# A list scheduler's table of durations: transposing DMAs, float16 splits, small operations and changes of product type

## The chip, the cores and the metric

The kernel runs on one core of a Trainium2 chip. The metric is device time in microseconds of one execution; the table below gives the median of three executions. The core's engines are TensorE (PE, with its weight loads shown apart as PEld), VectorE (DVE), ScalarE (ACT), GpSimd (POOL) and SyncE (SP), whose queue issues the DMAs here. Every engine runs its own instructions in the order in which they stand in the program and waits on semaphores for the others.

## What is computed

Attention over a local window and block summaries, then LayerNorm and a feed-forward network with a residual. B = 4, H = 8, S = 768, D = 64, so the model width is 512; the FFN goes from 512 to 2048 and back.

```python
block, window = (32, 16)
k_sum = k.reshape(B, H, nb, block, D).max(axis=3)
v_sum = v.reshape(B, H, nb, block, D).mean(axis=3)
scores_l = scale * np.matmul(q, k.transpose(0, 1, 3, 2))
mask_l = np.abs(pos[:, None] - pos[None, :]) < window
scores_s = scale * np.einsum('bhsd,bhnd->bhsn', q, k_sum) + np.log(block)
...
a = softmax(concat([where(mask_l, scores_l, -1e9), scores_s]))
x = a @ concat([v, v_sum])                      # heads side by side: (B, S, 512)
xn = (x - mu) / np.sqrt(var + 1e-06) * g_ln
out = x + np.maximum(xn @ w_ch1, 0.0) @ w_ch2
```

## The kernel before

The rows of all batches are cut into 24 tiles T of 128 rows. Attention runs in 48 steps t = 2T + hh, each for four heads of one tile; LayerNorm runs per tile, the FFN per group g of two tiles (12 groups), each in eight sections s = 8g + j of two blocks of 128 hidden columns.

Attention, t < 12 (batch 0): `early_qk` makes the scores s in float32 with products of 64 rows, `softmax` reduces and masks them on DVE and takes the exponential on ACT, `early_transp` turns the probabilities on PE (pp) and `early_pv` makes o. Before the first of them, `fetch_k0` loads the keys, `batch_k` takes their block maxima on DVE (kmax) and `batch_v0` makes the block means of the values as PE products v0 from value loads in_va. Attention, t ≥ 12: `load_q` and `load_k` split queries and keys into float16 halves (qhl; kh on ACT, kl on DVE from the staged ksg), `load_v` the values (v16), `qk` makes s from kh and kl, `softmax` writes p (DVE, with the row minimum mn; POOL scales mn; ACT the exponential), `transp` splits p into p16 on ACT and POOL and turns it with one transposing DMA on SP into pT, `pv` makes o on PE (12 products), reduces it on DVE into x and scales x on POOL. `batch(b)` prepares the next batch: maxima and sums of its keys, queries and values (bst, kmax, vsum, vm, vps), and `batch_vput` copies vsum into the value staging vst with small SP DMAs.

`ln` makes xn on DVE (bn_stats, bn_aggr, one product). `lnT` turns it: for T < 8 with PE transposes (tx), else with 16 transposes of 32x32 blocks on DVE (xn<-xn); ACT then rounds it to xth, and DVE (T < 8) or POOL makes the rest xtl. `g1(s)` makes h with 24 products, three (high·high, low weights, low x) for each of four parts and two blocks; ACT takes the ReLU and the high part hh, DVE the low part hl. `g2(s)` makes a with 12 products for each of the two tiles. An FFN section of group g needs both tiles of the group, that is xth and xtl of tile 2g + 1, whose attention ends with o of step 4g + 3: o19 is the last attention product ahead of h32, o23 of h40. The weights arrive as raw<-in_w (32 loads) and are turned into w on DVE and ACT (`conv_w`, four DVE instructions each, through wf).

Nothing is issued while this is recorded. Class `Plan` (line 68 on) records each operation with its predecessors (`record`), prices it (`cost`: its length in ns on its engine, and for a DMA the time of its transfer), and `issue` makes an order: a list scheduler places each engine's next ready operation by rank. The ranks begin with the longest path to the end plus a random offset of up to ±2000 ns for each step (`SEED`, `SPREAD`; `DRAWS` = 1) and are then taken from the ends of a schedule, forward and backward, `ROUNDS` = 24 times; the best of the forward ones is kept. `WAIT` and `SAME` are the delays between a predecessor and its follower, `ISSUE` = 450 ns the length of a DMA issue on SP, `SWITCH` = 93 ns a charge on PE, `port` makes DVE and POOL operations that read SBUF twice exclude one another in the plan. The instructions stand in the program in the order found, and the scheduler of the framework is off. All of them are issued from line 284, so the rows of the trace name no other line and are told apart by tiles.

Of the kernel before, what the change touches and what calls it, by code (L numbers as in the profile page):

```python
# [15 lines left out]
F32R = mybir.dt.float32r  # L16
F16 = mybir.dt.float16
# [7 lines left out]
P = 128  # L25
# [14 lines left out]
EH = 4  # L40
BS = 3
ROUNDS = 24
SEED, DRAWS = 2, 1
SPREAD = 2000.0
WARMQ = 4
WARMV = 4
# [17 lines left out]
class Plan:  # L64
# [58 lines left out]
    def record(self, engine, op, a, k):  # L123
        on_chip = lambda x: isinstance(x, bass.AP) and x.space != bass.MemoryType.DRAM
        outs = [x for x in (a[0], k.get("accum_out"), *a[7:8]) if on_chip(x)]
        ins = [x for x in (*a[1:7], *k.values()) if on_chip(x)]
        i, after = len(self.ops) - bool(self.joined), {}
        for aps, write in ((ins, False), (outs, True)):
            for x in aps:
                tile, *b = self.box(x)  # L130
                assert self.uses.get(tile, 1), tile
                if tile not in self.uses:
                    self.uses[tile] = []
                    if tile in self.prev:
                        for _, w, j in self.uses[self.prev[tile]]:
                            after[j] = after.get(j, False) or not w
                        self.uses[self.prev[tile]] = None
                elif tile in self.prev:
                    after.setdefault(self.uses[tile][0][-1], False)
                for c, w, j in self.uses[tile]:  # L140
                    if (write or w) and b[0] < c[1] and c[0] < b[1] and b[2] < c[3] and c[2] < b[3]:
                        after[j] = after.get(j, False) or not (write and w)
                self.uses[tile].append((b, write, i))
        busy, moving = self.cost(engine, op, a, k, ins, outs)
        columns = 0
        if engine == "tensor":
            columns = ({'matmul': 4, 'transpose': 2}[op] if ins[-1].dtype == F32 else 1) * math.prod(n for _, n in a[0].ap[1:]) * ins[0].ap[0][1] / P
        if self.joined:
            x = self.ops[i]
            x.calls.append((op, a, k))  # L150
            x.after.update(after)
            x.busy += busy
            x.columns += columns
        else:
            half = engine == "tensor" and ins[0].ap[0][1] == P // 2
            x = SimpleNamespace(engine=engine, calls=[(op, a, k)], after=after, busy=busy, moving=moving, columns=columns, stage=self.stage, port=self.port(engine, op, ins, outs), half=half)
            self.ops.append(x)
        x.after.pop(i, None)
        if self.joined is None:
            self.joined = True  # L160

    def cost(self, engine, op, a, k, ins, outs):

        free = lambda x: math.prod(n for _, n in x.ap[1:])
        n = max(free(x) for x in ins + outs) if engine != "tensor" else free(a[0])
        if engine == "sync":
            x = (outs + ins)[0]
            return self.ISSUE, x.ap[0][1] * free(x) * mybir.dt.size(x.dtype) / (200.0 if "transpose" in op else 360.0)
        if engine == "tensor":
            dt = ins[-1].dtype  # L170
            if dt == F32R:
                return 0.443 * max(n, 256) + 4.5, 0.0
            if dt == F16 or op == "transpose":
                return max((1 if dt == F16 else 2) * n / 2.4 + 3.0, 28.0), 0.0
            return (2 if ins[0].ap[0][1] > D else 1) * max(2 * n / 2.4 + 2.0, 100.0), 0.0
        psum = any(x.space == bass.MemoryType.PSUM for x in ins)
        pointers = sum(1 for x in ins[1:] if free(x) == 1)
        if engine == "scalar":
            extra = ("accum_out" in k) + sum(isinstance(k.get(x), bass.AP) for x in ("scale", "bias"))
            return n / 1.2 + (51 if psum else 93) + 93 * extra, 0.0  # L180
        if engine == "vector":
            fixed = {"transpose": 183, "tensor_tensor_reduce": 158}.get(op, 70)
            return n / (1.92 if op == "tensor_scalar" and not psum else 0.96) + fixed + 61 * (pointers > 0), 0.0
        if op == "tensor_scalar":
            return 180 + n + 61 * pointers + 300 * (n == 1), 0.0
        if op == "tensor_copy":
            return 120 + 3.33 * n, 0.0
        if op == "tensor_tensor":
            shifted = outs[0].offset // outs[0].ap[0][0] != ins[0].offset // ins[0].ap[0][0]
            return 517 if n == 1 else 40 + 2.1 * n + 110 * (shifted or outs[0].dtype == F32R), 0.0  # L190
        return 60 + 0.8 * n, 0.0

    @staticmethod
# [11 lines left out]
    def schedule(self, rank, after, back):  # L205

        count = len(self.ops)
        before = [[] for _ in range(count)]
        left = [len(x) for x in after]
        for i, x in enumerate(after):  # L210
            for j, wait in x:
                before[j].append((i, wait))
        ready, start, end = [0.0] * count, [0.0] * count, [0.0] * count
        free = dict.fromkeys(self.ENGINES, 0.0)
        coming, waiting = ({e: [] for e in self.ENGINES} for _ in range(2))
        ring, warm, columns, tick = 0.0 if back else self.FIRST, False, 0.0, 0.0
        port, half = 0.0, False
        for i in range(count):
            if not left[i]:
                heapq.heappush(coming[self.ops[i].engine], (0.0 if back else 1000.0, i))  # L220
        for _ in range(count):
            t, e = min(
                (free[e] if waiting[e] else max(free[e], coming[e][0][0]), k)
                for k, e in enumerate(self.ENGINES)
                if waiting[e] or coming[e]
            )
            e = self.ENGINES[e]
            while coming[e] and coming[e][0][0] <= t:
                i = heapq.heappop(coming[e])[1]
                heapq.heappush(waiting[e], (rank[i], i))  # L230
            i = heapq.heappop(waiting[e])[1]
            busy, moving = self.ops[i].busy, self.ops[i].moving
            if self.ops[i].port:
                t = port = max(t, port)
                port += busy
            if e == "tensor" and self.ops[i].half != half:
                half, t = self.ops[i].half, t + self.SWITCH
            if e == "tensor" and not back:
                while t >= tick + self.TICK:
                    warm, columns, tick = columns >= 3200, 0.0, tick + self.TICK  # L240
                busy *= 1 if warm else 2
                at, per = t, self.ops[i].columns / busy
                while t + busy >= tick + self.TICK:
                    columns += (tick + self.TICK - at) * per
                    warm, columns, tick = columns >= 3200, 0.0, tick + self.TICK
                    at = tick
                columns += (t + busy - at) * per
            start[i], free[e], end[i] = t, t + busy, t + busy
            if e == "sync":
                ring = max(ring, t if back else t + busy + self.SETUP) + moving  # L250
                if back:
                    free[e] = max(free[e], ring)
                end[i] = ring + (self.SETUP + busy if back else 0)
            for j, wait in before[i]:
                ready[j] = max(ready[j], end[i] + wait)
                left[j] -= 1
                if not left[j]:
                    heapq.heappush(coming[self.ops[j].engine], (ready[j], j))
        return start, end
# [744 lines left out]
```

## Time and profile before

| | |
|---|---|
| three executions, us | 682.6, 681.9, 684.57; median 682.6 |
| profiled execution, own time, us | 682.88 |
| its span, us | 680.8 |
| mean granted TensorE clock | 0.990 |
| PE busy, us (share) | 655.8 (96%) |
| DVE busy, us (share) | 511.7 (75%) |
| ACT busy, us (share) | 369.8 (54%) |
| POOL busy, us (share) | 218.6 (32%) |

The rows of the profile are of one execution. A row of instructions has the start in us, the busy time in us, the engine, line, operation, out<-in by tile names (without their numbers), shape and count, and in brackets the idle time of the engine just before and what ended it. The span starts with the first instruction and ends with the last; some 2.1 us lie around it.

### The profile page before, as it was taken

How to read it: one execution, taken by the hardware profiler on the slowest of the kernel's cores; microseconds unless marked ns; L12 is line 12 of the kernel's file. 1: busy time of each engine (PE TensorE's matmuls, PEld its weight loads, DVE VectorE, ACT ScalarE, POOL GpSimd, SP SyncE). 2: the span in 40 equal slices, each digit the busy share in tenths (PEclk: the TensorE clock that was granted, in tenths of full speed). 3: DMA queues.
4: the chain of work that ended last, by engine and by line, in shares of the span. 5: the costliest groups of instructions: out<-in, count | busy, mean ns of one | idle time of the engine just before them, and what ended most of it. 6: DMA issues, size and time to landing. Idle time of an engine off the chain costs nothing.

```text
span 680.8 us, 13615 instructions
## 1 busy us (share of the span) xinstructions
PE 655.8 (96%) x4641; PEld 577.8 (85%) x4641; DVE 511.7 (75%) x1370; ACT 369.8 (54%) x970; POOL 218.6 (32%) x421
## 2 busy tenths in 40 slices
PE   9959999999999999989999999899999999999998
PEld 6748898888988987878988888798989888989997
DVE  3899989877566899879999888898998574742211
ACT  3936788475566766666666555666664434311110
POOL 4211200233333444634444354355343332310000
PEclk9959999999999999999999999999999999999999
DMA  9990564446564655655664544564543321210000
GB/s 304 362 350 28 147 214 121 146 138 183 141 164 121 176 139 128 170 151 150 172 141 126 141 102 101 126 146 103 144 108 81 84 79 35 55 24 1 32 1 31
DMA packets 109495, 87.89 MB, mean 129 GB/s; under 512 B 63218, under 2 KB 93938, under 8 KB 109427
## 3 DMA queue, kind: packets, MB, share of 16 engines
q1 hardware_dynamic: 109426, 87.04, 47.0%
q8 instruction: 36, 0.59, 0.4%
q14 instruction: 33, 0.26, 0.1%
HBM read 66.27 MB, written 6.29 MB: 107 GB/s over the span
## 4 chain that ended last, share of the span: by engine, by line
PE 43%; DVE 18%; DMA 13%; ACT 6%; issue 6%; POOL 2%; SPq 1%; ACTq 0%; POOLq 0%; DVEq 0%
PE h L284 20%; PE a L284 19%; DVE xn L284 4%; DMA ksg<-in_kt 4%; DMA bst<-in_vs 3%; DVE kl L284 2%; DMA bst<-in_qa 2%; ACT p L284 2%; DVE hl L284 2%; PE s L284 2%; PE o L284 1%; DVE p L284 1%; DVE v L284 1%; DVE vsum L284 1%; DVE x L284 1%
## 5 line engine op out<-in xcount | busy, mean ns | idle before, releaser
L284 PE MATMUL h<-xth,w 128*128 128x256 f32 x1536 | 301.3, 286 | 0.9 <-ACT xth L284 0.7
L284 PEld LDWEIGHTS h<-xth,w 128*128 128x128 f32 x1536 | 246.0, 190 | 4.1 <-ACT xth L284 1.1
L284 PE MATMUL a<-w,hh 128*128 128x512 f32 (+1 forms) x768 | 241.6, 396 | 0.0
L284 PE MATMUL h<-xtl,w 128*128 128x256 f32 x768 | 216.9, 282 | 0.8 <-POOL xtl L284 0.7
L284 PEld LDWEIGHTS a<-w,hh 128*128 128x128 f32 x768 | 135.4, 188 | 24.2 <-issue 0.9
L284 PE MATMUL a<-w,hl 128*128 128x512 f32 (+1 forms) x384 | 149.9, 390 | 0.2 <-DVE hl L284 0.2
L284 PEld LDWEIGHTS h<-xtl,w 128*128 128x128 f32 x768 | 145.8, 190 | 3.3 <-POOL xtl L284 1.0
L284 DVE SCALAR_TENSOR_TENSOR hl<-h,hh 128x512 fp32r<-128x512 f32 x96 | 65.7, 685 | 71.6 <-ACT hh L284 71.0
L284 ACT ACTIVATE hh<-h 128x512 fp32r<-128x512 f32 x96 | 56.5, 588 | 97.3 <-PE a L284 39.3
L284 ACT ACTIVATE p<-p,mn,sv 128x184 f32<-128x184 f32 x144 | 76.5, 532 | 57.7 <-POOL mn L284 57.5
L284 PEld LDWEIGHTS a<-w,hl 128*128 128x128 f32 x384 | 72.2, 188 | 16.9 <-DVE hl L284 0.6
L284 POOL TENSOR_TENSOR p<-p,p 128x512 f16<-128x512 f32 x72 | 71.6, 1002 | 39.6 <-ACT p L284 39.0
L284 DVE STREAM_TRANSPOSE xn<-xn 32x128 f32<-32x128 f32 x256 | 77.5, 303 | 4.5
L284 ACT ACTIVATE kh<-ksg,sv 128x368 f16<-128x368 f32 x72 | 43.2, 599 | 50.5 <-POOL ksg L284 39.3
L284 DVE SCALAR_TENSOR_TENSOR kl<-ksg,sv,kh 128x368 f16<-128x368 f32 x72 | 50.3, 699 | 20.8 <-ACT kh L284 20.0
L284 POOL TENSOR_SCALAR mn<-mn,sv 128x2 f32<-128x2 f32 x72 | 30.7, 427 | 78.5 <-DVE mn L284 69.1
L284 DVE CUSTOM_DVE_ANT_0 p<-s,mask 128x184 f32<-128x184 f32 x144 | 44.7, 340 | 9.9 <-PE s L284 9.2
L284 ACT ACTIVATE bst<-bst 128x384 f32<-128x384 f32 (+2 forms) x55 | 32.5, 590 | 26.8 <-DMA bst<-in_qa 11.6
L284 POOL COPY ksg<-ksum 128x48 f32<-128x48 f32 x72 | 18.8, 261 | 84.1 <-DMA ksg<-in_kt 66.1
L284 DVE SCALAR_TENSOR_TENSOR v<-vst,sv,v 128x256 f16<-128x256 f32 x72 | 42.5, 612 | 1.7 <-ACT v L284 1.2
L284 DVE SCALAR_TENSOR_TENSOR wf<-raw,wf 128x512 uint32<-128x512 uint32 x64 | 41.8, 680 | 0.0
L284 POOL TENSOR_TENSOR x<-x,rc 128x256 f32<-128x256 f32 x36 | 25.2, 699 | 47.6 <-DVE x L284 44.0
(106 smaller groups left out, 818.3 us busy)
## 6 DMA issues: line engine op xcount, KB each, us to landing
raw<-in_w SPq DMA_DIRECT2D x32, 512.0 KB
ksg<-in_kt SPq DMA_DIRECT2D x72, 184.0 KB
qs<-in_qt SPq DMA_DIRECT2D x72, 128.0 KB
out_x<-x SPq DMA_DIRECT2D x23, 256.0 KB
vst<-in_va SPq DMA_DIRECT2D x36, 128.0 KB
bst<-in_ks SPq DMA_DIRECT2D x20, 192.0 KB
bst<-in_qa SPq DMA_DIRECT2D x15, 256.0 KB
bst<-in_vs SPq DMA_DIRECT2D x20, 192.0 KB
```

The source lines that it names most:

```text
L284: getattr(getattr(nc, self.ops[i].engine), op)(*a, **k)
```

## The change

Only the planner's table and the seed of its one draw change; every instruction of the program stays. A transposing DMA is priced at 1500 ns of SP's queue where every DMA was 450. On DVE the fixed part of `tensor_tensor_reduce` falls from 158 to 92 ns, an operation on four columns (rc and its reciprocal) gets 120 ns more, one that writes float16 (kl, v, qhl) 80 more. On POOL `tensor_tensor` gets 60 ns more. `half` had told products over 64 rows from all others; now it tells apart 64 rows (1), float16 (2) and the rest (0), and `SWITCH` is charged at each change of it except from 0 to 2.

```diff
-SEED, DRAWS = 2, 1
+SEED, DRAWS = 7, 1
...
-            half = engine == "tensor" and ins[0].ap[0][1] == P // 2
+            half = engine == "tensor" and (1 if ins[0].ap[0][1] == P // 2 else 2 * (ins[-1].dtype == F16))
...
-            return self.ISSUE, x.ap[0][1] * free(x) * mybir.dt.size(x.dtype) / (200.0 if "transpose" in op else 360.0)
+            return 1500.0 if "transpose" in op else self.ISSUE, x.ap[0][1] * free(x) * mybir.dt.size(x.dtype) / (200.0 if "transpose" in op else 360.0)
...
-            fixed = {"transpose": 183, "tensor_tensor_reduce": 158}.get(op, 70)
-            return n / (1.92 if op == "tensor_scalar" and not psum else 0.96) + fixed + 61 * (pointers > 0), 0.0
+            fixed = {"transpose": 183, "tensor_tensor_reduce": 92}.get(op, 70)
+            return n / (1.92 if op == "tensor_scalar" and not psum else 0.96) + fixed + 61 * (pointers > 0) + 120 * (n == 4) + 80 * (outs[0].dtype == F16), 0.0
...
-            return 517 if n == 1 else 40 + 2.1 * n + 110 * (shifted or outs[0].dtype == F32R), 0.0
+            return 517 if n == 1 else 100 + 2.1 * n + 110 * (shifted or outs[0].dtype == F32R), 0.0
...
             if e == "tensor" and self.ops[i].half != half:
-                half, t = self.ops[i].half, t + self.SWITCH
+                t += self.SWITCH if self.ops[i].half + half != 2 or not self.ops[i].half else 0
+                half = self.ops[i].half
```

The changed kernel issues from line 285. Three places of its order follow, first that of before, then the new one.

DVE at the start, around the second tile's LayerNorm (mv1 and xn3 are of tile 1; tx0 and tx1 are the PE transposes of tiles 0 and 1; wf and w are weights). Before:

```order
L284 TENSOR_TENSOR w2_2_272<-wf2_2_271,w2_2_272 128x512
L284 BN_AGGR mv1_156<-s6_1_155 128x2
L284 TENSOR_SCALAR wf3_1_274<-raw1_3_273 128x512
L284 SCALAR_TENSOR_TENSOR xn3_158<-x1_144,mv1_156,gb_74 128x512
L284 SCALAR_TENSOR_TENSOR wf3_1_274<-raw1_3_273,wf3_1_274 128x512
L284 TENSOR_SCALAR wf4_1_280<-raw1_4_279 128x512
L284 SCALAR_TENSOR_TENSOR wf3_1_274<-raw1_3_273,wf3_1_274 128x512
L284 TENSOR_SCALAR wf3_2_277<-raw2_3_276 128x512
L284 TENSOR_TENSOR xtl_0_132<-tx1_159,xth_0_131 128x4x128
```

Now:

```order
L285 ISA mn5_173 128x1
L285 BN_AGGR mv1_156<-s6_1_155 128x2
L285 TENSOR_SCALAR wf1_2_265<-raw2_1_264 128x512
L285 SCALAR_TENSOR_TENSOR wf2_1_268<-raw1_2_267,wf2_1_268 128x512
L285 SCALAR_TENSOR_TENSOR xn3_158<-x1_144,mv1_156,gb_74 128x512
L285 TENSOR_SCALAR rc5_180<-sum5_174 128x4
L285 TENSOR_TENSOR w1_2_269<-wf2_1_268,w1_2_269 128x512
L285 RECIPROCAL rc5_180<-rc5_180 128x4
L285 SCALAR_TENSOR_TENSOR wf1_2_265<-raw2_1_264,wf1_2_265 128x512
L285 TENSOR_SCALAR wf2_2_271<-raw2_2_270 128x512
L285 TENSOR_TENSOR xtl_0_132<-tx0_133,xth_0_131 128x4x128
```

xn3 now stands three instructions behind the score reductions of step 5 (fourteen before) and ahead of the first tile's xtl; the second tile's xtl follows ten instructions further, sixteen behind xn3 (four before). On PE and SP, ahead of this, of the seven products v0 none stands ahead of the score products s0 now (four before), and two ahead of s1 (all seven before); on SP the last of the four key loads is the sixth transfer (the tenth before), ahead of three value loads in_va that stood before it.

DVE where PE waits for the low keys of step 25 (x11 is the result of step 23, xn69 and xn73 are turned rows of two tiles). Before:

```order
L284 STREAM_TRANSPOSE xn69_751<-xn68_748 32x4x32 x5
L284 SCALAR_TENSOR_TENSOR kl25_0_838<-ksg25_0_836,sv2_728,kh25_0_837 128x368
L284 STREAM_TRANSPOSE xn69_751<-xn68_748 32x4x32 x7
L284 TENSOR_REDUCE x11_768<-o23_783 128x256
L284 SCALAR_TENSOR_TENSOR hl36_672<-h36_670,hh36_671 128x512
L284 STREAM_TRANSPOSE xn69_751<-xn68_748 32x4x32
L284 SCALAR_TENSOR_TENSOR qhl26_858<-qs78_857,sv2_728,qhl26_858 64x512
L284 SCALAR_TENSOR_TENSOR kl25_1_844<-ksg25_1_842,sv2_728,kh25_1_843 128x368
```

Now:

```order
L285 TENSOR_REDUCE x11_768<-o23_783 128x256
L285 SCALAR_TENSOR_TENSOR kl25_0_838<-ksg25_0_836,sv2_728,kh25_0_837 128x368
L285 SCALAR_TENSOR_TENSOR qhl26_858<-qs78_857,sv2_728,qhl26_858 64x512
L285 SCALAR_TENSOR_TENSOR v16_1_352<-vst1_78,sv2_728,v16_1_352 128x4x64
L285 BN_STATS s6_11_785<-x11_768 128x6
L285 SCALAR_TENSOR_TENSOR v16_1_352<-vst1_78,sv2_728,v16_1_352 64x4x64
L285 BN_AGGR mv11_786<-s6_11_785 128x2
L285 SCALAR_TENSOR_TENSOR hl38_678<-h38_676,hh38_677 128x512
L285 SCALAR_TENSOR_TENSOR xn72_788<-x11_768,mv11_786,gb_74 128x512
L285 SCALAR_TENSOR_TENSOR kl25_1_844<-ksg25_1_842,sv2_728,kh25_1_843 128x368
L285 STREAM_TRANSPOSE xn73_789<-xn72_788 32x4x32 x16
```

Tile 11's reduction and LayerNorm have moved ahead of step 25's keys, no transposes of the tile before stand here any more, and the 16 of tile 11 stand in one piece behind kl25_1.

SP around the transposing DMA of step 34 (vst is the value staging, vsum the block sums, ksg staged keys, qs staged queries). Before:

```order
L284 DMA vst1_78<-in_va 128x256
L284 DMA qs121_1177<-in_qt 64x512
L284 DMA vst1_78<-in_vb 32x256
L284 DMA vst1_78<-vsum3_1059 24x128 x2
L284 DMA ksg36_0_1162<-in_kt 128x368
L284 DMA_TRANSPOSE pT_34_1108<-p16_34_1107 128x12x128
L284 DMA ksg36_1_1168<-in_kt 128x368
```

Now:

```order
L285 DMA vst1_78<-vsum3_1059 24x128
L285 DMA_TRANSPOSE pT_34_1108<-p16_34_1107 128x12x128
L285 DMA qs121_1177<-in_qt 64x512
L285 DMA vst1_78<-in_va 128x256
L285 DMA ksg36_0_1162<-in_kt 128x368
L285 DMA qs121_1177<-in_qt 64x512
L285 DMA vst1_78<-in_vb 32x256
L285 DMA vst1_78<-vsum3_1059 24x128 x2
```

The pair of copies from vsum and the load of ksg36_0 have moved from ahead of the transposing DMA to behind it.

On PE, counted in the same way: between the last product of o19 and the first of h32 stood 48 h, 48 a, 16 s and 12 o products and now stand 36, 36, 8 and 12; the corresponding stretches of h40, h48 and h64 are shorter too, while between the last product of s20 and the first of s36 720 h products stand where 648 stood. Blocks of float16 products between others number 103 before and 102 now. The last instructions of every engine are the same.

## Rows read from the trace of the kernel before

**Rows 1.** Stretches (us): length, busy of PE, PEld, DVE, ACT, POOL; PEclk, DMA share, GB/s

```profile
0.00:17.00 17.00, 15.30 (x68) 10.61 (x68) 6.16 (x15) 5.73 (x18) 7.13 (x43) 1.00 0.91 304
34.00:51.00 17.00, 9.72 (x50) 8.20 (x50) 17.00 (x40) 6.67 (x16) 3.10 (x2) 0.60 1.01 351
51.00:255.00 204.00, 201.35 (x1433) 178.24 (x1432) 166.16 (x424) 137.40 (x386) 55.51 (x114) 1.00 0.52 143
255.00:425.00 170.00, 163.43 (x1186) 142.15 (x1185) 153.10 (x435) 106.96 (x269) 77.69 (x134) 1.00 0.55 138
252.28:268.89 16.61, 16.09 (x101) 12.72 (x101) 15.56 (x42) 9.79 (x25) 8.42 (x13) 1.00 0.46 115
```

**Rows 2.** What PE waited for, 255 to 430 us: total us, times, longest

```profile
PE o L284 <- DMA pT<-p: 4.5, 5, 2.2
PE s L284 <- DVE kl L284: 2.5, 4, 1.7
PE h L284 <- POOL xtl L284: 0.7, 1, 0.7
PE vps L284 <- DVE vm L284: 0.5, 1, 0.5
PE s L284 <- ACT kh L284: 0.3, 1, 0.3
PE a L284 <- DVE hl L284: 0.2, 1, 0.2
```

**Rows 3.** What DVE waited for in the first 34 us

```profile
DVE kmax L284 <- DMA spare<-in_ks: 8.8, 4, 4.5
DVE p L284 <- PE s L284: 2.7, 5, 0.9
```

**Rows 4.** DVE instructions at the start, around the second tile's xn and xtl

```profile
41.33 0.74 DVE L284 SCALAR_TENSOR_TENSOR xn<-x,mv,gb 128x512 f32<-128x512 f32 x1
...
43.90 0.69 DVE L284 TENSOR_TENSOR xtl<-tx,xth 128x512 fp32r<-128x512 f32 x1
```

**Rows 5.** PE instructions at the start, the transposes of the second tile

```profile
42.13 1.12 PE L284 MATMUL tx<-ident,xn 128*128 128x128 f32 x4 [5.79 <-DVE xn L284]
```

**Rows 6.** DVE instructions that make kl, a usual one and that of s25_1

```profile
299.46 0.60 DVE L284 SCALAR_TENSOR_TENSOR kl<-ksg,sv,kh 128x368 f16<-128x368 f32 x1 [2.34 <-ACT kh L284]
...
304.99 1.49 DVE L284 SCALAR_TENSOR_TENSOR kl<-ksg,sv,kh 128x368 f16<-128x368 f32 x1
```

**Rows 7.** POOL instruction beside the second of these

```profile
304.79 1.29 POOL L284 TENSOR_TENSOR xtl<-xn,xth 128x512 fp32r<-128x512 f32 x1 [0.38 <-ACT xth L284]
```

**Rows 8.** PE instruction that waited for it

```profile
306.53 0.24 PE L284 MATMUL s<-kl,qhl 128*128 128x184 f16 x1 [1.67 <-DVE kl L284]
```

**Rows 9.** SP's queue ahead of the transposing DMA of step 34

```profile
421.68 1.54 SPq L284 DMA_DIRECT2D vst<-vsum  x2
423.32 0.46 SPq L284 DMA_DIRECT2D ksg<-in_kt  x1
423.89 1.83 SPq L284 DMA_TRANSPOSE pT<-p  x1
```

**Rows 10.** PE instructions of step 34 that waited for it

```profile
428.19 0.74 PE L284 MATMUL o<-v,pT 128*128 128x128 f16 x12 [2.22 <-DMA pT<-p]
```

**Rows 11.** PE instructions: o19, the h32 product that waited, o23

```profile
248.83 0.74 PE L284 MATMUL o<-v,pT 128*128 128x128 f16 x12
...
271.06 0.39 PE L284 MATMUL h<-xtl,w 128*128 128x256 f32 x1 [0.69 <-POOL xtl L284]
...
295.55 0.74 PE L284 MATMUL o<-v,pT 128*128 128x128 f16 x12
```

**Rows 12.** POOL instruction that makes the last xtl ahead of h40

```profile
316.86 1.54 POOL L284 TENSOR_TENSOR xtl<-xn,xth 128x512 fp32r<-128x512 f32 x1 [2.32 <-ACT xth L284]
```

**Rows 13.** The chain of waits, 454 to 463 us: start us, us, what

```profile
454.50 4.28 PE h L284 x36
...
459.12 2.84 PE a L284 x12
```

More of the change, by code (lines that the diff above doesn't have):

```diff
@@ L216, in schedule @@
         ring, warm, columns, tick = 0.0 if back else self.FIRST, False, 0.0, 0.0
-        port, half = 0.0, False
+        port, half = 0.0, 0
         for i in range(count):
```

## The prediction, made before the changed kernel ran

> **What bounds the kernel now.** I read the table of busy time by stretch first. TensorE (PE) is busy nearly everywhere, so the time can only fall where PE stands idle. Its idle time is the length of a stretch less its busy time: 7.3 us between 34 and 51 us (17.00 − 9.72), where the granted clock is 0.60 of full speed on average; 2.7 us between 51 and 255 us, spread over 204 us; 6.6 us between 255 and 425 us [rows 1]. Then I read what PE waited for. Between 255 and 430 us the waits add up to 8.7 us: 4.5 for the transposed probabilities pT that a DMA brings, 2.5 for kl, the low half of the keys that VectorE (DVE) makes, and smaller ones for xtl, vm, kh and hl [rows 2]. (One of them, 2.2 us, lies just behind 425 us [rows 10].) After 430 us the view of waits has no row at all: there PE has products of the FFN to fill every gap. So two places can pay, the start (until the first h product) and the middle, where a wait of PE is a wait of the kernel.
>
> The change alters only the planner's table, so the same instructions run and only their order differs. What each misplaced instruction costs is therefore a question of these two places.
>
> **The start.** PE's idle 5.8 us ends with the transposes tx of the second tile, which wait for xn [rows 5]. On DVE xn runs at 41.33 and the second xtl at 43.90 us [rows 4]; conversions of weights stand ahead of and between them, and DVE is busy all of the 17 us [rows 1]. In the changed order three instructions stand between the last score reduction and xn, where fourteen stood (twelve of them conversions); but sixteen, mostly the same conversions, now stand between xn and the second xtl, where four did. The wait moves from xn to xtl, then, and the first h products come when DVE has done the work ahead of the second xtl. Net work ahead of it, counted from the order: one more weight instruction (0.6), one reduction of kmax (0.5) and two pairs for rc (0.5) less one short conversion (0.3), about +1.3 us, an estimate. Against that DVE idles less before: in the first 34 us it waited 8.8 us for the keys' loads and 2.7 us for score products [rows 3]. The changed order issues the key loads ahead of three value loads of 262 KB each (at the 304 GB/s of the first stretch [rows 1], 2.6 us), and puts the score products s0 and s1 ahead of nearly all products of the block means. Saved idle time: 0 at worst; at best 2.7 and 2.1 of the 2.6 us, that is 4.8; I take 2.6, the loads alone. First h: −2.6 + 1.3 = **−1.3 us**, bounds +1.3 and −3.5.
>
> **The middle, pT.** The longest wait, 2.22 us, is the 12 o products of step 34 waiting for pT_34 [rows 10]. Its transposing DMA takes SyncE's queue from 423.89 for 1.83 us, directly behind two small copies of vsum (1.54 us) and a load of keys (0.46 us) [rows 9]: 2.0 us of queue ahead of the one transfer that is urgent. The changed order puts pT_34 ahead of the pair and of ksg36_0. What is late next is the POOL split that feeds it. I let this wait go but for 0.3 us, and of the other four (2.3 us together) I leave 0.7, since a table that says 1500 instead of 450 makes the planner see the queue blocked: 4.5 becomes 1.0; bounds 0 and 4.5. Behind it stand now qs121, a value load, ksg36_0 and the pair, delayed by at most its 1.83 us; PE waited for none of what these feed but kl and kh [rows 2].
>
> **The middle, kl.** The 1.67 us wait of s25_1 [rows 8] ends with kl25_1, which took 1.49 us where a usual one takes 0.60 [rows 6]. It started at 304.99, and POOL ran xtl from 304.79 to 306.08 [rows 7]: kl moved only when POOL had finished. In the changed order kl25_1 stands behind xn72 and ahead of 16 transposes, and kl25_0 and qhl26 right behind the reduction of x11. I let 2.8 us (kl and kh) become 0.7; bounds 0 and 2.8, and beyond that if POOL's splits now meet more of them.
> The Trainium skill ("SBUF — State Buffer", section "SBUF: two separate sides") says that VectorE and GpSimd take a shared port pair as an exclusive lock for a whole instruction, and the loser blocks fully. The trace agrees: 1.49 against 0.60 us. The new table prices kl at a constant, with no such wait in that number; by the rule the 2.5 us of kl would stay, and the sum would be 678 instead of 676.
>
> **The middle, the LayerNorm chain.** Group 4's first h (h32) must wait for the second tile of its input: from the end of o19 (248.83 + 0.74 = 249.57) to the h32 product that waited for xtl (271.06) are 21.5 us [rows 11]; DVE has of it the stretch from the reduction of x9 at 252.28 to the last transpose at 268.89 us, 42 instructions with 15.56 us of work, 0.37 each [rows 1]. In the changed order 14 instructions of other steps leave that stretch and 3 come: −11 × 0.37 = −4.1 us, so 17.4 us if the rest of the chain stays, and 14.3, an estimate, if the reduction (now 2.7 us behind o19's end) starts at once and half a microsecond of queueing goes. But PE's work between o19 and h32 falls too: 48 h, 48 a, 16 s and 12 o products become 36, 36, 8 and 12. An h product takes 4.28/36 = 0.119 us, an a product 2.84/12 = 0.237 [rows 13]: 17.1 us of these become 12.8, and with the short s and o products, some 0.05 us each, 18.5 becomes 13.7 us. A stall of 0.6 to 3.7 us. For h40 the distance falls from 21.8 to 15.1; its chain, now 22.1 us (296.29 to 318.40) [rows 11, 12], loses ten instructions, 3.7 us, to 18.4 at most. For h48 and h64 the distances become 16.4 and 18.2 us. I take 1.5 us for all four, near the low end, since a chain may also lose its queueing; bounds 0 and 9.2 (3.7 + 3.3 + 2.0 + 0.2 with 18.4 us for the last two).
> What pays for this: between the last product of s20 and the first of s36 stand 720 h products where 648 stood, 8.6 us more FFN work beside the same work of the other engines, so fewer gaps for PE.
>
> Sum of the middle: 8.7 us before; 1.0 + 0.7 + 1.5 and 0.3 for the rest (vm, hl) = 3.5 after: **−5.2 us**, bounds −8.7 and, with the chains at 9.2, +2.5. The 2.7 us between 51 and 255 us [rows 1] I leave as they are (±2). The new rule on product types: changes to and from float16 products number 103 before and 102 after; one fewer is worth at most one product's 0.1 us: **−0.1**. The last instructions of all engines are the same: 0.
>
> The profiled execution took 682.88 us, 680.8 of span and 2.1 around it; it is 0.3 above the median of the runs, 682.6. 682.9 − 1.3 − 5.2 − 0.1 = 676.3; less 0.3 for the median's level: **676.0 us**.
>
> **Rivals.** *Better:* all of the middle's waits go and the start gives its 3.5: 682.6 − 8.7 − 3.5 = 670.4. For it: nothing waited after 430 us, where FFN work is at hand. Against: the four shorter distances.
> *No change:* the waits are of a sort that the table does not hold (kl held up by POOL [rows 6, 7], queues behind a landing transfer), so a new order has new ones of the same size: 682.6 − 1.3 − 0.1 = 681.2, or 682.5 without the start. For it: the table before was no worse in the first 255 us, and PE idled only 2.7 us in 204 there.
> By the rule of the Trainium skill on the port pair (same page and section) the kl part of this rival holds; the trace agrees for kl25_1 [rows 6, 7].
> *Slower:* the LayerNorm chain. If taking instructions out of DVE's stretch shortens the chain only to 20 us, because DVE then waits in the stretch for its inputs, the four stalls are 6.3 + 4.9 + 3.6 + 1.8 = 16.6 instead of 1.5: 676.0 + 15.1 = 691. It decides from a chain of some 18 us (8.8 us of stalls, near 683) and passes 686 at 18.7. For it: 17.4 and 18.4 by the instructions alone; against: the last 3 us of both are queueing, which the order can remove.
> *Not what it says:* the order differs also because the one random draw is another (seed 7, offsets up to ±2000 ns on every step). The rule for float16 changes their number by one, so it does nothing on the chip. The gain may be the draw's, the table's or both; the time would be the same, but each alone would not give it.
>
> **How the numbers follow.** Forecast 0.50, better 0.14, no change 0.23, slower 0.13. A measurement of this kernel can tell about 0.5% from no change: faster is below 679.2, slower above 686.0. The forecast and the better case are nearly all faster, of the no-change case little; a quarter of the slower rival (chain under 18.7) falls inside the bound: faster 0.64, same 0.25, slower 0.11. The range must leave out no more than 0.2: from 669.5 (the better case and 0.9 us of the first 255 us) to 684.0, which takes in no change and the mild end of the chain's stalls.
>
> **What would show it.** In the changed kernel's profile the first h products start when the second xtl has run, near 42.6 us instead of 43.9; PE's wait for pT between 255 and 430 us falls under 1.5 us and that for kl under 1; h waits for xtl at h32 and h40, 0.5 to 3 us each; no waits after 430 us. A single 3 us stall at each of the four groups' first h would make the slower rival right; s waits for kl with kl over 1 us beside a POOL split, the no-change one. A first h later than 44 us would show that the conversions ahead of xtl cost more than the loads gave. What would make all of it wrong is a gap in the first 255 us that the trace of before does not have.

## The result, and the profile after

The changed kernel took 674.28 us, median of four runs (672.41 to 674.73), against 682.25 for the kernel before in the same comparison: a ratio of 0.9872 with a 95% interval of 0.9841 to 0.9902, 8.0 us less. 676.0 had been predicted. Its profiled execution took 674.68 us, with a span of 672.9 and a granted clock of 0.990 on average, as before.

The stretches that answer to [rows 1], with the columns explained there:

```profile
34.00:51.00 17.00, 9.21 (x48) 8.26 (x49) 17.00 (x37) 7.01 (x17) 1.17 (x2) 0.60 0.97 333
51.00:255.00 204.00, 201.33 (x1434) 179.12 (x1432) 163.61 (x421) 135.53 (x379) 59.53 (x112) 1.00 0.52 143
255.00:425.00 170.00, 167.13 (x1206) 147.46 (x1206) 148.38 (x407) 104.02 (x261) 74.73 (x126) 1.00 0.54 131
```

PE is idle 2.9 us between 255 and 425 us where it was 6.6; DVE has 4.7 us less to do there (148.4 against 153.1); that work stands later, beside the last FFN sections (between 510 and 612 us DVE is busy 76.6 us where it was 62.6). The stretch from 51 to 255 us is as before. What PE waited for between 255 and 430 us, answering to [rows 2]:

```profile
PE o L285 <- DMA pT<-p: 1.3, 1, 1.3
PE s L285 <- ACT kh L285: 0.8, 1, 0.8
PE s L285 <- DVE kl L285: 0.4, 1, 0.4
PE a L285 <- DVE hl L285: 0.4, 1, 0.4
```

2.9 us in four waits instead of 8.7 in thirteen. After 430 us there is none, as before. A wait costs more than the idle time listed, since the modelled end of a product lies behind the start of the next in an unbroken row (an h product is listed 0.28 us long, and the next one starts 0.12 us after it). Counted from start to start, the thirteen gaps of before were 10.9 us longer than the usual spacing, the four of after 3.5: **7.4 of the 8.0 us** are here, and the start gives most of the rest.

The start, answering to [rows 4, 5], DVE and then PE:

```profile
34.96 0.75 DVE L285 SCALAR_TENSOR_TENSOR xn<-x,mv,gb 128x512 f32<-128x512 f32 x1
...
43.42 0.69 DVE L285 TENSOR_TENSOR xtl<-tx,xth 128x512 fp32r<-128x512 f32 x1
```

```profile
35.76 0.92 PE L285 MATMUL tx<-ident,xn 128*128 128x128 f32 x4
37.36 0.58 PE L285 MATMUL h<-xth,w 128*128 128x256 f32 x1 [0.68 <-ACT xth L285]
44.17 0.58 PE L285 MATMUL h<-xtl,w 128*128 128x256 f32 x1 [6.22 <-DVE xtl L285]
```

xn comes 6.4 us sooner, the second xtl only 0.5 us. PE's wait moved from tx to the first xtl product and is 6.2 us long instead of 5.8.

### The profile page after: what moved, and what is told of

Its sections match the earlier page's. It is cut to its first block, busy times and chain, and to the rows that moved or that the text cites. A ratio compares the mean times of both kernels' runs of the same rounds, so it can differ in the third digit from the quotient of the medians.

```text
span 672.9 us, 13587 instructions
## 1 busy us (share of the span) xinstructions
PE 652.1 (97%) x4641; PEld 577.5 (86%) x4641; DVE 514.5 (76%) x1370; ACT 370.0 (55%) x970; POOL 225.0 (33%) x421
## 4 chain that ended last, share of the span: by engine, by line
PE 81%; DVE 7%; DMA 6%; ACT 3%; issue 2%; POOL 1%; SPq 1%; ACTq 0%; DVEq 0%; POOLq 0%
PE h L285 35%; PE a L285 34%; PE o L285 5%; PE s L285 4%; DMA pT<-p 1%; DVE xn L285 1%; DMA bst<-in_qa 1%; DVE wf L285 1%; ACT p L285 1%; PE v L285 1%; DMA qs<-in_qt 1%; DMA blk<-in_blocks 1%; SPq L285 1%; PE last L285 1%; DMA ksg<-in_kt 1%
## 5 line engine op out<-in xcount | busy, mean ns | idle before, releaser
L285 ACT ACTIVATE p<-p,mn,sv 128x184 f32<-128x184 f32 x144 | 76.6, 534 | 39.7 <-POOL mn L285 38.9
L285 POOL TENSOR_TENSOR p<-p,p 128x512 f16<-128x512 f32 x72 | 73.6, 1034 | 46.7 <-ACT p L285 46.0
L285 DVE SCALAR_TENSOR_TENSOR kl<-ksg,sv,kh 128x368 f16<-128x368 f32 x72 | 50.3, 699 | 12.4 <-ACT kh L285 11.8
L285 POOL TENSOR_SCALAR mn<-mn,sv 128x2 f32<-128x2 f32 x72 | 25.0, 348 | 77.5 <-DVE mn L285 69.0
L285 ACT ACTIVATE bst<-bst 128x384 f32<-128x384 f32 (+2 forms) x55 | 32.4, 590 | 27.0 <-DMA bst<-in_qa 16.3
L285 DVE SCALAR_TENSOR_TENSOR v<-vst,sv,v 128x256 f16<-128x256 f32 x72 | 44.8, 636 | 0.3
L285 POOL TENSOR_TENSOR x<-x,rc 128x256 f32<-128x256 f32 x36 | 27.4, 762 | 42.7 <-DVE x L285 39.1
```

What stands on the lines that cost most here:

```text
L285: getattr(getattr(nc, self.ops[i].engine), op)(*a, **k)
```

## Experiments: which part of the change did it

The change has three ingredients: the price of a transposing DMA (1500 ns of SP's queue), the other prices, and the draw (seed 7). The first of these is a correction: in the trace of the kernel before, the 36 transposing DMAs hold SP's queue for 1.49 us in the median (1.29 to 2.27). Six runs take the ingredients apart.

**The price of the DMA put back**, all else new:

```diff
-            return 1500.0 if "transpose" in op else self.ISSUE, ...
+            return self.ISSUE, ...
```

> The changed kernel with one number put back: a transposing DMA is planned at 450 ns of SP's queue again; seed 7 and all other new prices stay. Between the last product of s20 and the first of s36 the order then has 612 h products, where the changed kernel has 720 and the kernel before 648. Theory P (pacing: this one number makes the planner space the attention steps wider and put more FFN work between them): the waits of PE between 255 and 430 us come back, 7 us or more, and the time is 681 to 684 us. Rival D (the draw of seed 7 made the gain): 673 to 676 us. Rival R (the other new durations made it): 673 to 677 us.

695.04 us, 1.0153 times the kernel before (1.0112 to 1.0193). The rivals D and R, at 677 us or less, are out. The middle is as theory P has it, with these waits of PE between 255 and 430 us, 8.6 us in all:

```profile
PE o L285 <- DMA pT<-p: 2.9, 2, 1.6
PE s L285 <- DVE kl L285: 2.2, 6, 0.8
PE h L285 <- DVE mv L285: 2.0, 1, 2.0
PE vps L285 <- DVE vm L285: 1.0, 1, 1.0
```

But the time is 11 us beyond the top of P's range: the first 255 us are worse too, and after 430 us PE waits 2.1 us where the kernel before waits for nothing. **This price alone**, on the old table and draw:

> The kernel before with this one number alone changed: 1500 ns for a transposing DMA, seed 2 and all other prices as before. 696 h products stand between s20 and s36 (648 before, 720 in the changed kernel). Theory P: 674 to 678 us, the waits of PE between 255 and 430 us under 4 us. Rival D (the draw): 681 to 684 us. Rival R (the other durations): 680 to 684 us.

679.91 us, 0.9947 (0.9928 to 0.9965), and in the middle only

```profile
PE s L284 <- DVE kl L284: 1.8, 4, 0.5
PE h L284 <- DVE hl L284: 0.7, 1, 0.7
```

The middle gains what the changed kernel gains there, and the start gives half of it back, so the time ends 2 us above P's range. **The draw alone**, and **the new prices with the old draw** (only the seed differs, `SEED, DRAWS = 7, 1` and `2, 1`):

> The kernel before with seed 7 for its one draw, no price changed. 624 h products stand between s20 and s36. Theory P: no gain, 680 to 685 us, waits of 7 us or more between 255 and 430 us. Rival D (the draw): 673 to 676 us.

> The changed kernel with seed 2 put back, all new prices kept. 696 h products stand between s20 and s36. Theory P: 673 to 677 us, as with seed 7, waits under 4 us between 255 and 430 us. Rival D (the draw): 681 to 684 us.

692.39 us, 1.0127 (1.0094 to 1.0159), and 683.46 us, 1.0005 (0.9981 to 1.0029). Neither gains, so D, under which seed 7 alone would bring 673 to 676 us, is out. P missed the first run: it gave 680 to 685 us with 7 us or more of waits in the middle, and the run was 7 us slower with 5.9 us of waits. P's time for the second was wrong too (673 to 677): its middle is the best of all (1.4 us idle), but the first 140 us are the worst. **The price of the DMA with the new draw on the old table, and the other new prices with the old draw:**

> The kernel before with 1500 ns for a transposing DMA and seed 7, no other price changed. Here the number does not change the pacing: 636 h products stand between s20 and s36 (696 with seed 2, 648 in the kernel before). Theory P in its narrow form (what counts is how much FFN work the order leaves between the attention steps): the waits of PE between 255 and 430 us stay at 6 us or more, 686 to 693 us. Rival Q (what counts is that the planner knows the queue of SP to be blocked, so the transposing DMAs are issued sooner): the waits for pT in that stretch fall under 1 us, and the time is 4 us or more under that of the old table with seed 7 (692.4), 684 to 688 us.

> The changed kernel with 450 ns for a transposing DMA and seed 2. 636 h products between s20 and s36. If the issue number alone makes the middle: idle time of PE between 255 and 430 us 7 us or more (with 1500 ns and seed 2: under 3), and the time above that of the new table with seed 2 (683.5) unless the start is better, 684 to 695 us. If the other new durations do part of it: 5 us or less idle.

682.94 us, 1.0009 (0.9984 to 1.0034), and 688.05 us, 1.0084 (1.0065 to 1.0103). The first of these contradicts P in its narrow form: the spacing of the attention steps is the old one, yet the waits are 4.6 us, those for pT 0.6, and the time is 1.2% under that of seed 7 alone. That is the sign of rival Q, whose time (684 to 688 us) was 1 us too high. In the second, 6.0 us of idle time in the middle lie between the two conditions that were set (7 or more, 5 or less), so by them it decides nothing.

Times as ratios to the kernel before in the same comparison:

| | seed 2 | seed 7 |
|---|---|---|
| old prices, 450 | 1 | 1.0127 |
| old prices, 1500 | 0.9947 | 1.0009 |
| new prices, 450 | 1.0084 | 1.0153 |
| new prices, 1500 | 1.0005 | 0.9872 |

The step from 450 to 1500 gains in all four pairs, by 0.5 to 2.8%. The other prices lose in three of four (once within the intervals), the seed too; only the three together give the result. PE's idle time by stretch (the stretch less its busy time, from the profiled executions) says where it goes. (The profiled execution of new, 1500, seed 2 lies 3 us above that kernel's median, so its first number is somewhat too high.)

| kernel | h products, s20 to s36 | idle 0 to 140 us | 140 to 255 | 255 to 430 | 430 to 612 |
|---|---|---|---|---|---|
| before | 648 | 12.4 | 0.3 | 8.8 | 0.1 |
| old, 1500, seed 2 | 696 | 15.9 | 0.0 | 2.5 | 0.6 |
| old, 450, seed 7 | 624 | 17.3 | 1.6 | 6.2 | 3.4 |
| old, 1500, seed 7 | 636 | 17.7 | 0.5 | 4.6 | 0.6 |
| new, 450, seed 2 | 636 | 19.1 | 0.6 | 6.0 | 0.3 |
| new, 1500, seed 2 | 696 | 19.3 | 0.1 | 1.4 | 1.4 |
| new, 450, seed 7 | 612 | 16.3 | 3.6 | 9.0 | 2.2 |
| after (new, 1500, seed 7) | 720 | 13.9 | 0.8 | 2.9 | 0.0 |

In the middle the idle time goes with the price: 1.4 to 4.6 us with 1500, 6.0 to 9.0 with 450. The first 140 us go with none of the three: they lie between 12.4 and 19.3 us, and both kernels of this case happen to have a good start, the mixtures do not. That every changed price simply draws the order of the start anew fits these numbers, but no run isolates it. The middle and the start are not all of it either: the two slowest kernels of the table (450, seed 7) also idle 5.0 and 5.8 us between 140 and 255 us and behind 430 us, where the kernel before idles 0.4. The rows do not add up to the times, since a wait costs more than its idle time and PE's clock differs too (last section).

**The rule on float16 products taken out** of the changed kernel (`half` is 1 for 64 rows, else 0):

> The changed kernel without the rule on float16 products (half is 1 for products over 64 rows and 0 for all others, as before). 708 h products stand between s20 and s36. Theory: the rule does nothing on the chip by itself, so the middle stays: waits of PE between 255 and 430 us under 4 us; the first 140 us are drawn anew, as every change of a price does, so 674 to 684 us, by the start alone. Rival (the rule is what saves time in the middle): waits of 6 us or more there.

678.06 us, 0.9941 (0.9918 to 0.9964), 2.6 us idle in the middle: the rule has no part in the middle; the 0.7% by which this kernel stands behind the changed one lie mostly in its first 140 us (14.9 idle against 13.9, and a second fall of PE's clock near 86 us, to 0.66 of full speed from 86 to 90 us).

**Not the queue but the landing** is priced 1050 ns longer in the old table:

```diff
-... else self.WAIT[a]) for a, (j, y) in ...
+... else self.WAIT[a] + 1050 * ("transpose" in self.ops[j].calls[0][0] and a == "sync")) for a, (j, y) in ...
```

> The kernel before, seed 2, with the 1050 ns put not on SP's queue but on the way from the transposing DMA to its reader (a longer landing, the issue stays 450). 648 h products stand between s20 and s36, as in the kernel before, so the order is not spaced wider. If it is the blocked queue in the plan that helps (theory Q, and the wider spacing it led to): idle time of PE between 255 and 430 us stays at 7 us or more, 681 to 688 us. If any later pT in the plan helps: under 5 us idle, 675 to 680 us.

691.87 us, 1.0141 (1.0113 to 1.0169), worse than expected by 4 us, with 8.2 us idle in the middle. The waits are instructive:

```profile
PE s L284 <- DVE kl L284: 4.2, 10, 0.8
PE s L284 <- ACT kh L284: 3.2, 3, 2.4
PE o L284 <- DMA pT<-p: 0.3, 1, 0.3
```

With the readers of pT planned later the wait for pT is nearly gone (0.3 us for 4.5), but the keys are late instead and the sum is nearly the same, 7.7 us for 8.7. So 1050 ns more on the way of pT alone do not help on this draw, and the price of 1500 did. In the planner that price does two things: the queue is occupied longer, and the transfer lands up to 1050 ns later. This run has the second without the first; the occupied queue without the later landing was not run.

## Experiments: single waits moved by hand

These take an order as it is and move one to three instructions; nothing is planned again.

**In the order before, pT_34 goes ahead on SP:**

```diff
+DMA_TRANSPOSE pT_34<-p16_34
 DMA vst1<-vsum3 x2
 DMA ksg36_0<-in_kt
-DMA_TRANSPOSE pT_34<-p16_34
```

> The order before with one move, by hand: on SP the transposing DMA of step 34 stands ahead of the two copies from vsum and of the load ksg36_0, nothing else moves. If the queue of SP holds it up (the step of the prediction): it is issued about 1.3 us sooner (its input is ready some 1.3 us before its issue), the wait for pT falls from 2.2 to about 1 us and the time by 1 us, 0.15%. If the chain that feeds it (the reduction on DVE and the split on POOL) is what is late: issue and wait move by less than 0.4 us, the time not at all.

```profile
423.14 1.48 SPq L304 DMA_TRANSPOSE pT<-p  x1
424.67 1.65 SPq L304 DMA_DIRECT2D vst<-vsum  x2
426.43 0.46 SPq L304 DMA_DIRECT2D ksg<-in_kt  x1
```

```profile
426.98 0.74 PE L304 MATMUL o<-v,pT 128*128 128x128 f16 x12 [0.48 <-DMA pT<-p]
...
434.15 0.36 PE L304 MATMUL h<-xth,w 128*128 128x256 f32 x1 [1.81 <-DVE hl L304]
```

The queue did hold pT_34 up: the wait falls from 2.22 [rows 10] to 0.48 us, further than the 1 us expected. But the load of the keys now comes later, POOL and, behind it, ACT wait for it, and on DVE the low half, and hl behind it, start late:

```profile
429.88 0.65 DVE L304 SCALAR_TENSOR_TENSOR kl<-ksg,sv,kh 128x368 f16<-128x368 f32 x1 [4.02 <-ACT kh L304]
```

In the kernel before this kl started at 427.23 (0.5 us of the difference is there ahead of the moved transfer already). The wait of 1.81 us for hl was not there before; the time is 683.30 us, 1.0021 (1.0003 to 1.0038): nothing gained.

**In the order before, kl25_1 goes ahead of qhl26 on DVE:**

```diff
+SCALAR_TENSOR_TENSOR kl25_1<-ksg25_1,sv2,kh25_1
 SCALAR_TENSOR_TENSOR qhl26<-qs78,sv2,qhl26
-SCALAR_TENSOR_TENSOR kl25_1<-ksg25_1,sv2,kh25_1
```

> The order before with one move: on DVE kl25_1 stands ahead of qhl26. If POOL holds DVE up while it runs xtl (theory L): kl25_1 now runs at about 304.1 us for 0.60 us and the 1.67 us wait of s25_1 is gone; qhl26, also of two inputs from SBUF, now takes the delay instead, about 1.5 us or more in place of 0.87; the time falls by about 1.5 us if nobody waits for qhl26. If kl25_1's own 1.49 us have another reason: it is as long in its new place, and qhl26 stays at 0.87.

DVE, POOL and PE:

```profile
303.87 0.93 DVE L303 SCALAR_TENSOR_TENSOR kl<-ksg,sv,kh 128x368 f16<-128x368 f32 x1 [0.79 <-ACT kh L303]
304.83 1.66 DVE L303 SCALAR_TENSOR_TENSOR qhl<-qs,sv,qhl 64x512 f16<-64x512 f32 x1
```

```profile
304.42 1.52 POOL L303 TENSOR_TENSOR xtl<-xn,xth 128x512 fp32r<-128x512 f32 x1
```

```profile
304.85 0.24 PE L303 MATMUL s<-kl,qhl 128*128 128x184 f16 x1 [0.72 <-DVE kl L303]
```

The delay belongs to whoever stands beside POOL's xtl: kl25_1 is down from 1.49 to 0.93 us, and qhl26, 0.87 us before, takes 1.66 and ends 0.55 us after xtl. The Trainium skill ("SBUF — State Buffer", section "SBUF: two separate sides") states an exclusive lock on a shared port pair for such pairs; these rows agree. The wait of s25_1 falls from 1.67 to 0.72 us, and the 0.95 us saved come back 3 us later as a wait that the kernel before did not have:

```profile
307.62 0.74 PE L303 MATMUL o<-v,pT 128*128 128x128 f16 x12 [0.93 <-DMA pT<-p]
```

So the time does not fall by the 1.5 us expected: 681.97 us, 1.0009 (0.9988 to 1.0030), with 8.7 us idle between 255 and 430 us, 8.8 before.

**In the changed order, the second xtl goes nine conversions forward on DVE** (behind the first xtl); in the second kernel hh0 on ACT and hl0 on DVE go forward too:

> The changed order with one move by hand: on DVE the second tile's xtl (which PE waits for 6.2 us at the start) stands nine conversions earlier, right behind the first tile's xtl. Theory V (DVE's conversions bound the start, the wait only changes its place): the first h products start about 5.4 us sooner, near 38.7 us, and PE then waits for hl0 (on DVE at 52.1 us) and the weights: gain at most 1.3 us, 672.9 to 674.5 us. Rival (the wait itself is the price): 5 us, 669 us.

> As the run before, and hh0 on ACT and hl0 on DVE moved up too, hl0 eight instructions. Theory V: the next thing late is w1_4 (its low half is ready at 53.4 us, PE asks for it some 5 us sooner than in the changed kernel, where it had 4.3 us of slack): gain 1 to 3.5 us, 670.8 to 673.3 us. Rival (hl0 was the only thing late): 5 us, 669 us.

674.54 us (0.9895, 0.9876 to 0.9914) and 674.73 us (0.9887, 0.9866 to 0.9908): both the time of the changed kernel. That fits theory V for the first kernel (a gain of 1.3 us at most) and is less than it gave the second (1 to 3.5 us); the rivals' 669 us is out. The first xtl product starts at 40.94 and 40.25 us instead of 44.17, but neither theory named what comes next. In the second kernel, PE's waits in the first 140 us begin so:

```profile
PE o L311 <- DMA vst<-in_vb: 3.3, 1, 3.3
```

Until 51.70 us the o products of the early attention wait for a load of values that stood far behind the weights on SP; in the first kernel the same wait is 4.0 us. PE's clock falls again behind it (from 50 to 58 us the granted clock is 0.79 of full speed here, 0.59 in the first kernel). The DMAs are busy 0.97 of the time between 34 and 51 us in the changed kernel, and in these two runs the wait for DVE that was taken away was handed to a load.

## Why the prediction held, point by point

- **The start** was forecast at −1.3 us and gave −0.5. The mechanism was right: xn comes early, and the wait moves to the second xtl. The mis-sized term is the idle time saved, taken as 2.6 us, which came to 1.9: DVE's wait for the key loads fell from 8.8 to 6.4 us and that for the score products from 2.7 to 2.0 [rows 3], 3.1 together, but new waits came, the rows of after being

```profile
DVE kmax L285 <- DMA spare<-in_ks: 6.4, 2, 4.1
DVE p L285 <- PE s L285: 2.0, 3, 0.9
DVE rc L285 <- ACT p L285: 0.9, 1, 0.9
```

  DVE is busy 23.3 us of the first 34 where it was 21.4: 1.9 us of gain, less the 1.3 of added work.
- **pT**, from 4.5 to 1.0 forecast: 1.3 came. For step 34 the reading of the queue was right, as the move by hand shows; the prediction excepted kl and kh from what nobody waits for behind pT_34, and it is the keys' load, by way of kl and the hl behind it, that took the gain back in that run. In the changed kernel it was harmless: the 1.3 us are one wait, at 304.88 us, of another step.
- **kl and kh**, from 2.8 to 0.7: 1.2 came. kl25_1 runs at 313.24 us for 0.59 us, and nobody waits. The no-change rival counted kl held up by POOL among the waits that the planner cannot see; that was wrong, since the planner's `port` keeps such pairs apart in the plan, though on the chip, where the times differ from the plan's, this one met.
- **The LayerNorm chains**, 1.5 us of stalls forecast: none is listed. From the end of o19 to xtl it takes 15.2 us (21.5 before), of which the reduction starts 0.36 us after o19's end where it was 2.7. That is near the lower end of the stretch that was reckoned (14.3 to 17.4): most of the queueing went with the instructions. But the stall also failed to come because PE's work was priced too low: between o19 and h32 PE goes on until 268.60 us, 15.0 us after o19's end with one wait of 0.36 us in them, where the prediction summed 13.7. With 13.7 a chain of 15.2 us would have stalled PE by 1.5. The slower rival is refuted; h32, h40, h48 and h64 follow their xtl without a wait of 0.3 us or more, though with nearly nothing to spare:

```profile
267.19 1.59 POOL L285 TENSOR_TENSOR xtl<-xn,xth 128x512 fp32r<-128x512 f32 x1
```

```profile
268.60 0.28 PE L285 MATMUL h<-xth,w 128*128 128x256 f32 x1
268.84 0.39 PE L285 MATMUL h<-xtl,w 128*128 128x256 f32 x1
```

- **The sum of the middle**, −5.2 forecast, is −5.8 in listed idle time and −7.4 from start to start. The mis-sized part is the price of a wait: some 0.17 us more than is listed for each. That the listed sum came so near is in part luck: pT, kl and kh came 0.8 us above their forecast, and the 1.5 us of stalls did not come at all.
- **The float16 rule**: nothing in the middle, as forecast. **The rival that the change doesn't do what it says** was right in part: of the ingredients only the price of the DMA is a gain by itself, and a gain of 0.5%. What the prediction did not see is that the gain in the middle goes with that one number, and that the good start is luck: no ingredient by itself brings it. It forecast the order at hand from its rows, which needs neither.

What stays open: why the planner spaces the steps wider when SP's queue is priced longer with three of the four combinations of prices and seed, and not with the old prices and seed 7; and how the middle gained there without it. That is a matter of the planner's search, and no run isolates it.

## What to carry to other kernels

Where DVE is busy 90% of a stretch or more, moving the late instruction did not remove the wait: in four orders with one to three instructions moved by hand it came back elsewhere. What went with waits under 3 us in the middle, in all four planned orders that have them, was more of PE's own work between the steps (696 to 720 h products for 648); one order with 636 had 4.6 us. When a planner's price is corrected, test that price over several draws: here one of the corrected prices gained in all four pairs, and the rest of the correction moved the time between 1.4% down and 0.8% up. Price a transfer that occupies a queue as occupation of that queue: the same 1050 ns priced only as a longer way lost 1.4% on the one draw tried.

## What was not expected of the hardware

A short wait in the early part can be followed by a fall of the clock that costs as much again. In the run with pT_34 moved, whose first part is the order of before, PE waited 1.6 us at 125 us for an ACT copy (1.3 in the kernel before), and then:

```profile
124.00:126.00 2.00, 1.35 (x6) 0.75 (x4) 1.22 (x3) 0.11 (x1) 0.69 (x1) 1.00 0.40 136
126.00:128.00 2.00, 1.06 (x9) 1.06 (x10) 2.00 (x7) 1.65 (x4) 1.26 (x2) 1.00 0.01 4
128.00:130.00 2.00, 2.00 (x14) 2.00 (x14) 2.00 (x4) 1.05 (x5) 1.13 (x3) 0.66 0.53 133
130.00:132.00 2.00, 2.00 (x11) 1.98 (x11) 1.81 (x5) 0.83 (x3) 1.20 (x2) 0.50 0.53 183
```

The last column but two is the granted clock: it falls to 0.50, the lower of its two levels (1.2 GHz), after the wait and is back at 132 us, while the kernel before, after its wait of 1.3 us, keeps 1.00. In 4 us at 0.66 and 0.50 PE does 2.3 us of work. Up to 421 us the two kernels have the same order, so this is a difference between two executions and not between two orders. Of the kernels run here only before, after, the old table with seed 7 and the move of kl25_1 have no second fall of the clock between 54 and 354 us in their profiled execution. So the clock is a part of what a start costs, but it does not explain why the starts differ: the old table with seed 7 has no second fall and idles 17.3 us in its first 140 us all the same.
